# Score matmuls of a decode-attention kernel: 24 written-out matmuls a half against two register-addressed loops

## The chip, the cores and the metric

The kernel runs on one core of a Trainium2 chip. The metric is device time in microseconds (us) from the first to the last instruction of the program on that core; three timed runs of the kernel before gave 1981.87, 1982.41 and 1983.38 us. The engines that matter here are TensorE (PE in the profile; PEld is its weight loads), VectorE (DVE), ScalarE (ACT) and SyncE (SP), which issues nearly all the transfers. Each engine has its own instruction stream, and the streams meet only through semaphores.

## The reference: four layers of one-token attention

One token of width 640 goes through four attention layers, A, B, A, B, each with a residual. A layer normalises the token, projects it to 32 query heads of 192, scores each query against 8192 cached keys, takes a softmax, sums the cached values with these weights, and projects back to 640. All inputs are bf16.

```python
def _B_ref(x, k_cache, v_cache, wq, wo):
    q = (x @ wq).reshape(B, Sq, H, Dh).transpose(0, 2, 1, 3)
    scores = einsum("bhqd,bhkd->bhqk", q, k_cache) * (Dh ** -0.5)
    p = softmax(scores, axis=-1)
    o = einsum("bhqk,bhkd->bhqd", p, v_cache)
    return o.transpose(0, 2, 1, 3).reshape(B, Sq, H * Dh) @ wo

x = x + _A_ref(layernorm(x), ...)
x = x + _B_ref(layernorm(x), ...)
x = x + _A_ref(layernorm(x), ...)
x = x + _B_ref(layernorm(x), ...)
```

The A and the B caches are each 32 heads x 8192 rows x 192 numbers for keys and the same for values. All of it is read once per layer, apart from a few tensors kept on the core, so the kernel moves about 849 MB.

## The kernel before

**Tiling.** Heads are taken two at a time: 16 pairs a layer, 64 in all. A pair's keys are one 128-partition tile of 128 rows x 192 numbers per partition (64 partitions for each head), and so are its values. Each is split in two halves, u = 0 and u = 1, of 3.1 MB. Halves live in a pool of eight slots on the core. A planner in Python lists all transfers in order (`plan`), picks the slots that come free earliest, and makes each transfer wait on SP's queue for the last reader of its slot. Most keys and values come as one transfer of 6.3 MB into two neighbouring slots.

**The work of a pair**, in the order of the list `steps`:

- `products(p, u)` for both halves. VectorE multiplies the key half in place by the query, in four quarters of 48 of the 192 columns (line 599, "pool <- pool, q_sb"). TensorE then sums the products over the 192 columns, eight columns at a time: 24 matmuls against an identity matrix, each 128 x 512, added up in the PSUM bank S0 or S1. The first is an ordinary `matmul` (line 612), which also loads the identity as weights; the other 23 go through the helper `matmul_held` (line 58), which keeps the weights that are loaded. The first six wait for quarter 0 (`PE.wait(chunks[0])`), the next six for quarter 1, and so on. The last one signals a semaphore, which frees the slot of the key half and releases the reduction.
- `softmax(p)`. VectorE reduces the eight columns left in S0 and S1 (line 621), takes the maximum (lines 623 and 630, with a small TensorE matmul at line 626 between them), and ScalarE takes the exponentials (line 636).
- `values(p)`. TensorE multiplies the weights by the value tile, 48 matmuls with 16 weight columns each, in four column groups (lines 678 and 58), into the accumulator O.
- `gather(p)`. VectorE adds up eight slices of O (lines 696 and 697), TensorE folds the partitions (line 710), and ScalarE writes the pair's output row (line 721).

**Order.** The streams are written out by hand, and each engine does its part strictly in that order. On VectorE the next pair's products come after this pair's `gather`, which waits for this pair's `values`, which waits for this pair's score matmuls. On TensorE the score matmuls of u = 1 come after those of u = 0. So a pair is one chain through VectorE, TensorE, VectorE, ScalarE, TensorE and VectorE, and pairs do not overlap except in their transfers. Every five pairs, output weights `wo` are applied (line 538), and between layers the query weights `wq` are.

**The queue object.** `Queue.op` adds an instruction to an engine's stream, with its waits ahead of it; with `signal=False` no semaphore is signalled. `emit` plays the list to the engine.

Of the kernel before, what the change touches and what calls it, by code (L numbers as in the profile page):

```python
# [55 lines left out]
def matmul_held(t, out, lhsT, rhs, start, stop, size=128, column=0):  # L56

    return t.add_instruction(mybir.InstMatmult(  # L58
        name=t.bass.get_next_instruction_name(), engine=mybir.EngineType.PE,
        ins=[t.lower_ap(rhs), t.lower_ap(lhsT, for_matmul_weights=True)], outs=[t.lower_ap(out)],  # L60
        start_tensor_calc=start, stop_tensor_calc=stop, tile_size=(128, size), tile_position=(0, column), ldweights=False))
# [7 lines left out]
def build(nc, A_x, A_k, A_v, A_wq, A_wo, B_x, B_k, B_v, B_wq, B_wo, out):  # L69
    _, H, SK, DH = A_k.shape  # L70
# [8 lines left out]
    QD = DH // 4  # L79
    R = 512 // JU  # L80
# [17 lines left out]
    with ExitStack() as ctx:  # L98
        def sb(name, shape, dt):
            return ctx.enter_context(nc.sbuf_tensor(name, shape, dt))  # L100
# [4 lines left out]
        def sem(name):  # L105
            return ctx.enter_context(nc.semaphore(name))

        ident = sb("ident", [P, P], BF16)
# [51 lines left out]
        Su = [(use["S0"],), (use["S1"],)]  # L160
# [6 lines left out]
        PE = Queue(sem("pPE"))  # L167
# [7 lines left out]
        e = PO.op(lambda g: g.memset(ident[:], 0.0))  # L175
# [6 lines left out]
        e = PO.op(lambda g: g.memset(mask, 0.0))  # L182
        for t in range(G):
            e = PO.op(lambda g, t=t: g.affine_select(
                out=mask, in_=mask, compare_op=ALU.not_equal, fill=1.0,
                base=-32 * t, pattern=[[-1, 2], [-2, VK]], channel_multiplier=1), e)
# [13 lines left out]
        def first_load(kind, l, p):  # L200

            n = (kind, pair(l, p))
            if l >= 2 and n in KEPT[l - 2]:
                return (l - 2, ORDER[l - 2]["pairs"].index(n[1]))
            return (l, p)

        def stays(kind, l, p):
            return l < 2 and (kind, pair(l, p)) in KEPT[l]
# [17 lines left out]
        for l in range(NL):  # L226
# [8 lines left out]
            for p in range(NPAIR):  # L235
# [17 lines left out]
                if p < NPAIR - 2:  # L253
# [8 lines left out]
                    if p + 1 in (PAIRS_W, 2 * PAIRS_W):  # L262
                        b = (p + 1) // PAIRS_W - 1
# [132 lines left out]
        def need(n):  # L396

            while n not in landed:
                m = plan[issued[0]]
                issued[0] += 1  # L400
                landed[m] = transfer(m)
            return landed[n]
# [45 lines left out]
        def layer(l, ev_z, ev_true):  # L448
# [7 lines left out]
            if l == 2:  # L456
                busy(2)
            e = DV.op(lambda v: v.scalar_tensor_tensor(out=nv[:], in0=mv[:, 0:1], scalar=mv[:, 0:1], in1=mv[:, 1:2],
                                                       op0=ALU.mult, op1=ALU.subtract))
            e = DV.op(lambda v: v.tensor_scalar(vs[:], nv[:], -float(DH), float(DH) * EPS, ALU.mult, ALU.add), e, last["rs"])  # L460
# [6 lines left out]
            if l < 2:  # L467
                e = need(("wq", l, 0))
# [4 lines left out]
            else:  # L473
                e = ev_first[l - 2]
                q_first = wq0[l - 2]
            PE.wait(e)
            for c in range(DC):
                for h in range(2):
                    e = PE.op(lambda t, c=c, h=h: t.matmul(
                        QM[64 * h:64 * h + 64, 0:DH], lhsT=xb[:, c:c + 1].broadcast_to([P, 64]),  # L480
                        rhs=q_first[:, c, h * DH:(h + 1) * DH], start=(c == 0), stop=(c == DC - 1)),
                        signal=(c == DC - 1 and h == 1), bank=QMu)
# [106 lines left out]
            def products(p, u):  # L589
                nk = ("k",) + first_load("k", l, p) + (u,)  # L590
                nt = ("t", l, p, u) if stays("k", l, p) else nk
                kin = slot[place[nk]].rearrange("p (j d) -> p j d", d=DH)
                k3 = slot[place[nt]].rearrange("p (j d) -> p j d", d=DH)
                qi = (l * NPAIR + p) % 2
                DV.wait(need(nk), need(nt), ev_q[p])
                chunks = []
                for c in range(4):
                    d0 = c * QD
                    e = DV.op(lambda v, d0=d0: v.tensor_tensor(  # L599
                        k3[:, :, d0:d0 + QD], kin[:, :, d0:d0 + QD],  # L600
                        q_sb[qi][:, d0:d0 + QD].unsqueeze(1).broadcast_to([P, JU, QD]), ALU.mult))
                    chunks.append(e)
                last["q"][qi] = chunks[-1]
                S = SP_[u]
                PE.wait(last["S"][u], ev_const)
                for c in range(4):
                    PE.wait(chunks[c])
                    for r in range(QD // R):
                        d0 = c * QD + r * R
                        fin = c == 3 and r == QD // R - 1  # L610
                        e = PE.op(lambda t, d0=d0, fin=fin: (
                            t.matmul(S[:, :], lhsT=ident[:], rhs=k3[:, :, d0:d0 + R], start=True, stop=fin) if d0 == 0 else  # L612
                            matmul_held(t, S[:, :], ident[:], k3[:, :, d0:d0 + R], False, fin)), signal=fin, bank=Su[u])
                freed[nt] = ev_S[p, u] = e

            def softmax(p):
# [109 lines left out]
            for n in [n for n in steps if n[1] == l]:  # L726
                if n[0] == "m":
                    products(*n[2:])
                elif n[0] == "s":
                    softmax(n[2])  # L730
# [36 lines left out]
            if l + 1 == NL:  # L767
                a = slot[place[("wo", 3, 2)]][0:33, 0:HD]
                return a, AC.op(lambda c: c.activation(a, YR, ACT.Copy), ev_y, last["oT"], bank=YBu)
            ev_z = DV.op(lambda v: v.tensor_tensor(z[:], xc[:], YB[:, 0:DC], ALU.add), ev_y, ev_xc, bank=YBu)  # L770
            e = DV.op(lambda v: v.tensor_tensor(x_true[:], x_true[:], YB[:, 0:DC], ALU.add), ev_y, ev_true, bank=YBu)
# [5 lines left out]
        e = SP.op(lambda s: s.dma_start(out[0, 0].rearrange("(h n) -> h n", h=2), ev_z[0:33:32, :]), ev_true, sem=semOUT, inc=16)  # L777
# [54 lines left out]
```

## Time and profile before

| What | Value |
|---|---|
| median of three timed runs | 1982.41 us |
| profiled execution, its span | 1982.1 us |
| DMA queue q1, share of 16 DMA engines over the span | 99.6 % |
| HBM read, mean rate | 848.36 MB, 428 GB/s |
| VectorE busy | 1201.2 us (61 %) |
| TensorE matmul busy | 1288.6 us (65 %) |
| ScalarE busy | 139.9 us (7 %) |
| products on VectorE, line 599 | 512 of 1753 ns, 861.1 us |
| score matmuls, lines 612 and 58 | 3072, 851.3 us busy |

The busy shares are averages, and a matmul's end is modelled, so that 65 % for TensorE is not a measure of how near it is to its limit. The waits between engines, and the times at which one pair's instructions follow another's, say more. In the profile's lists, an arrow "<-" in a group's name stands between what is written and what is read; after a wait it stands ahead of what ended it. An engine with a q after its name is that engine's sequencer, the part that reads instructions and handles moves, branches and semaphores itself.

### The profile page before, as it was taken

What the parts mean: (1) busy time and instruction counts of PE and PEld (TensorE: products, weight loads), DVE (VectorE), ACT (ScalarE), POOL (GpSimd) and SP (SyncE); (2) the same over time, 40 slices, a digit from 0 to 9 for tenths busy, and PEclk for the clock granted to TensorE, in tenths of its full rate; (3) what the DMA queues carried; (4) which work ended last, traced back from release to release, by engine and by line L of the source; (5) the groups of instructions that cost most, each with busy time, mean ns of one, the idle gap of its engine ahead of it and who ended that gap; (6) DMA issues with size and microseconds to landing.
All of it is one profiled execution on the core that took longest, in us unless ns stands there. A gap on an engine that the chain in (4) does not pass through costs nothing.

```text
span 1982.1 us, 13748 instructions
## 1 busy us (share of the span) xinstructions
PE 1288.6 (65%) x8248; PEld 146.4 (7%) x3160; DVE 1201.2 (61%) x1376; ACT 139.9 (7%) x462; POOL 4.5 (0%) x23
## 2 busy tenths in 40 slices
PE   3567476666466666666785676675776766657658
PEld 0001001000100100100020010010001001000001
DVE  3566467467166657556745565665764775665656
ACT  0000000000000000000010000000000100000000
POOL 0000000000000000000000000000000000000000
PEclk9787776778677777777887877878787888777779
DMA  9999999999999999999999999999999999999998
GB/s 414 438 431 430 431 436 432 430 430 429 435 432 433 434 430 432 429 435 433 426 407 426 425 426 426 432 430 431 434 429 427 435 431 433 433 432 431 433 433 367
DMA packets 26930, 849.25 MB, mean 428 GB/s; under 512 B 3058, under 2 KB 3188, under 8 KB 3828
## 3 DMA queue, kind: packets, MB, share of 16 engines
q1 hardware_dynamic: 26724, 848.38, 99.6%
q8 instruction: 45, 0.74, 0.2%
q14 instruction: 17, 0.14, 0.0%
q10 hardware_dynamic: 144, 0.00, 0.0%
HBM read 848.36 MB, written 0.00 MB: 428 GB/s over the span
## 4 chain that ended last, share of the span: by engine, by line
DMA 67%; DVE 17%; PE 15%; ACT 1%; issue 0%; SPq 0%
DMA pool<-in_B_k_cache_dram 27%; DMA pool<-in_A_v_cache_dram 20%; DVE pool L599 15%; DMA pool<-in_A_k_cache_dram 14%; PE S L58 6%; DMA pool<-in_B_v_cache_dram 6%; PE OY L58 5%; PE OY L678 3%; DVE acc L697 1%; ACT p_sb L636 1%; DVE s_sb L621 1%; PE S L612 0%; DVE m_bf L623 0%; PE OY L538 0%; PE QM L626 0%
## 5 line engine op out<-in xcount | busy, mean ns | idle before, releaser
L599 DVE TENSOR_TENSOR pool<-pool,q_sb 128x3072 bf16<-128x3072 bf16 x512 | 861.1, 1753 | 229.5 <-DMA pool<-in_B_k_cache_dram 133.5
L58 PE MATMUL S<-pool,ident 128*128 128x512 bf16 x2944 | 789.5, 425 | 19.5 <-DVE pool L599 17.6
L710 PE MATMUL TB<-acc,small 128*1 128x192 f32 x240 | 82.7, 495 | 212.0 <-DVE acc L697 212.0
L58 PE MATMUL OY<-pool,p_sb 128*16 128x512 bf16 x1920 | 202.7, 498 | 0.0
L696 DVE TENSOR_SCALAR acc<-OY,small 128x192 f32<-128x192 f32 x64 | 26.7, 418 | 287.5 <-PE OY L58 256.3
L678 PE MATMUL OY<-pool,p_sb 128*16 128x512 bf16 (+1 forms) x1216 | 148.2, 495 | 69.5 <-DMA pool<-in_A_v_cache_dram 63.5
L612 PE MATMUL S<-pool,ident 128*128 128x512 bf16 x128 | 61.8, 483 | 201.3 <-DVE pool L599 201.2
L697 DVE SCALAR_TENSOR_TENSOR acc<-OY,small,acc 128x192 f32<-128x192 f32 x424 | 177.1, 418 | 14.9
L621 DVE TENSOR_REDUCE s_sb<-S 128x64 f32<-128x512 f32 x128 | 88.0, 688 | 69.7 <-PE S L58 69.7
L527 ACT ACTIVATE q_sb<-QM 128x192 bf16<-128x192 f32 x60 | 19.9, 331 | 944.0 <-PE QM L521 944.0
L721 ACT ACTIVATE rows<-TB,small 1x192 bf16<-1x192 f32 x120 | 43.2, 406 | 596.3 <-PE TB L710 596.3
L692 DVE RECIPROCAL small<-TB 1x2 f32<-1x2 f32 x64 | 11.2, 175 | 94.5 <-PE TB L651 75.3
L636 ACT ACTIVATE p_sb<-s_sb,small 64x128 bf16<-64x128 f32 x128 | 55.7, 435 | 161.2 <-DVE small L630 160.4
L612 PEld LDWEIGHTS S<-pool,ident 128*128 128x128 bf16 x128 | 12.9, 101 | 676.2 <-DVE pool L599 604.4
L651 PE MATMUL TB<-small,ones 128*1 128x2 f32 x120 | 11.4, 165 | 74.1 <-ACT p_sb L636 74.1
L678 PEld LDWEIGHTS OY<-pool,p_sb 128*16 128x16 bf16 (+1 forms) x1216 | 39.8, 107 | 217.3 <-issue 138.8
L626 PE MATMUL QM<-ident,m_bf 128*64 128x64 bf16 x128 | 14.0, 216 | 54.4 <-DVE m_bf L623 53.9
L710 PEld LDWEIGHTS TB<-acc,small 128*1 128x1 f32 x240 | 19.8, 101 | 310.8 <-DVE acc L697 284.0
L630 DVE TENSOR_REDUCE small<-QM 128x1 f32<-128x64 f32 x64 | 14.4, 225 | 35.2 <-PE QM L626 35.2
L521 PEld LDWEIGHTS QM<-rows,one_b 1*64 1x64 bf16 x120 | 6.2, 100 | 347.0 <-issue 341.1
L538 PE MATMUL OY<-oT,pool 128*128 128x1 bf16 x675 | 28.6, 178 | 1.9 <-ACT oT L584 1.9
L538 PEld LDWEIGHTS OY<-oT,pool 128*128 128x128 bf16 x675 | 27.8, 131 | 3.8 <-ACT oT L584 2.5
(74 smaller groups left out, 215.2 us busy)
## 6 DMA issues: line engine op xcount, KB each, us to landing
pool<-in_B_k_cache_dram SPq DMA_DIRECT2D x28, 6144.0 KB, 37.9
pool<-in_B_v_cache_dram SPq DMA_DIRECT2D x28, 6144.0 KB, 33.5
pool<-in_A_v_cache_dram SPq DMA_DIRECT2D x27, 6144.0 KB, 27.5
pool<-in_A_k_cache_dram SPq DMA_DIRECT2D x34, 3072.0 KB, 20.5
pool<-in_A_k_cache_dram SPq DMA_DIRECT2D x14, 6144.0 KB, 36.4
pool<-in_A_v_cache_dram SPq DMA_DIRECT2D x10, 3072.0 KB, 14.7
pool<-in_B_k_cache_dram SPq DMA_DIRECT2D x8, 3072.0 KB, 22.5
pool<-in_A_wo_dram SPq DMA_DIRECT2D x6, 2400.0 KB, 21.9
```

The lines of the kernel that those rows point to most:

```text
L58: return t.add_instruction(mybir.InstMatmult(name=t.bass.get_next_instruction_name(), engine=mybir.EngineType.PE, ins=[t.lower_ap(rhs), t. ...
L527: lambda a: a.activation(q_sb[i][:], QM[:, 0:DH], ACT.Copy), e, last["q"][i], bank=QMu)
L538: e = PE.op(lambda t, i=i, c=c, f=y_first[0], fin=n[0] == "wol" and i == k - 1: t.matmul(YB[:, c:c + 1], lhsT=t3[:, i, c:D:DC], rhs=o[:, i ...
L599: e = DV.op(lambda v, d0=d0: v.tensor_tensor(k3[:, :, d0:d0 + QD], kin[:, :, d0:d0 + QD], q_sb[qi][:, d0:d0 + QD].unsqueeze(1).broadcast_t ...
L612: t.matmul(S[:, :], lhsT=ident[:], rhs=k3[:, :, d0:d0 + R], start=True, stop=fin) if d0 == 0 else
L621: lambda v, u=u: v.tensor_reduce(s[:, u * JU:(u + 1) * JU], SP_[u][:].rearrange("p (j r) -> p j r", r=R), AX.X, ALU.add), ev_S[p, u], last ...
L636: ev_p[p] = AC.op(lambda a, h=h, r=r: a.activation(p_sb[par][r, :, h], s[r, :], ACT.Exp, bias=negm[par][r, 0:1], accum_out=l_col[par][r, h ...
L678: t.matmul(o, lhsT=x, rhs=y, start=f, stop=fin) if c == 0 else
L696: v.tensor_scalar(acc[:], O[:, 0:DH], pick[:, 0:1], None, ALU.mult) if i == 0 else
L697: v.scalar_tensor_tensor(out=acc[:], in0=O[:, i * DH:(i + 1) * DH], scalar=pick[:, i:i + 1], in1=acc[:], op0=ALU.mult, op1=ALU.add)), e if ...
L710: e = PE.op(lambda t, h=h: t.matmul(TB[96:97, C_O + h * DH:C_O + (h + 1) * DH], lhsT=half[:, h:h + 1], rhs=acc[:], start=True, stop=True), ...
L721: last["TO"] = last["row_written"] = AC.op(lambda a, h=h: a.activation(orow[:, o0 + h * DH:o0 + (h + 1) * DH], TB[96:97, C_O + h * DH:C_O ...
```

## The change

In `products`, the 24 score matmuls of a half are written as two loops that run on TensorE's own sequencer. The first part does the ordinary first matmul (columns 0 to 7) and then a loop of 11 turns, for columns 8 to 95; the second part is a loop of 11 turns for columns 96 to 183 and one last matmul that ends the accumulation and signals. One turn holds one `matmul_held` whose moving operand is addressed by a register. There are two waits instead of four: the first part waits for quarter 1 (`chunks[1]`), the second for quarter 3 (`chunks[3]`). The number of matmuls, their operands and their order stay the same.

```diff
                 PE.wait(last["S"][u], ev_const)
-                for c in range(4):
-                    PE.wait(chunks[c])
-                    for r in range(QD // R):
-                        d0 = c * QD + r * R
-                        fin = c == 3 and r == QD // R - 1
-                        e = PE.op(lambda t, d0=d0, fin=fin: (
-                            t.matmul(S[:, :], lhsT=ident[:], rhs=k3[:, :, d0:d0 + R], start=True, stop=fin) if d0 == 0 else
-                            matmul_held(t, S[:, :], ident[:], k3[:, :, d0:d0 + R], False, fin)), signal=fin, bank=Su[u])
+                def scores(t, a, b):
+
+                    def one(d, start, stop):
+                        x = k3[:, :, bass.ds(d, R)]
+                        if start:
+                            return t.matmul(S[:, :], lhsT=ident[:], rhs=x, start=True, stop=stop)
+                        return matmul_held(t, S[:, :], ident[:], x, False, stop)
+
+                    if a == 0:
+                        one(0, True, False)
+                        a = R
+                    end = b - R if b == DH else b
+                    with t.Fori(a, end, R) as d:
+                        one(d, False, False)
+                    return one(end, False, True) if b == DH else None
+
+                PE.wait(chunks[1])
+                PE.op(lambda t: scores(t, 0, DH // 2), signal=False, bank=Su[u])
+                PE.wait(chunks[3])
+                e = PE.op(lambda t: scores(t, DH // 2, DH), bank=Su[u])
                 freed[nt] = ev_S[p, u] = e
```

Built into instructions, a turn of the loop is four on TensorE's stream: one that does four register operations at once (it works out the operand's address), the matmul, a register addition (the loop's counter), and a compare-and-branch. Ahead of each loop stand a register move, which sets the counter, and a branch. In the second part the wait for quarter 3 sits on that register move. The written-out form has a plain matmul for each of them and nothing else. The program has 256 such loops: two for each of 128 halves. The streams of the other engines are the same as before.

## The prediction

> **What bounds the kernel now.** I read the page first, then the waits, then the timeline of one pair, then the rows of the sequencers. The page's top, slices and queues:
>
> ```profile
> span 1982.1 us, 13748 instructions
> ...
> DMA  9999999999999999999999999999999999999998
> ...
> q1 hardware_dynamic: 26724, 848.38, 99.6%
> q8 instruction: 45, 0.74, 0.2%
> ```
>
> The transfers are the bound: their engines are busy in every fortieth of the span, 99.6% overall. Nothing in the change moves fewer bytes of data, so the kernel can only stay or lose. What it can absorb is read from the view of waits, in the rows where compute waits for a transfer (total us, times, longest):
>
> ```profile
> DVE pool L599 <- DMA pool<-in_B_k_cache_dram: 133.5, 30, 13.4
> DVE pool L599 <- DMA pool<-in_A_k_cache_dram: 94.6, 27, 9.8
> ...
> PE OY L678 <- DMA pool<-in_A_v_cache_dram: 63.5, 21, 10.9
> ...
> PE QM L479 <- DMA pool<-in_B_wq_dram: 12.8, 1, 12.8
> ...
> PE OY L678 <- DMA pool<-in_B_v_cache_dram: 6.0, 4, 3.5
> ```
>
> That is 310 us of slack, about 4.8 us for each of 64 pairs. The timeline shows how one pair looks where no transfer is waited for (start us, us):
>
> ```profile
> 1572.85 13.43 DVE L599 TENSOR_TENSOR pool<-pool,q_sb 128x3072 bf16<-128x3072 bf16 x8
> ...
> 1575.06 6.94 PE L58 MATMUL S<-pool,ident 128*128 128x512 bf16 x23
> ...
> 1586.34 1.46 PE L58 MATMUL S<-pool,ident 128*128 128x512 bf16 x6 [0.21 <-DVE pool L599]
> ...
> 1587.83 0.69 DVE L621 TENSOR_REDUCE s_sb<-S 128x64 f32<-128x512 f32 x1 [0.94 <-PE S L58]
> ...
> 1592.63 0.63 PE L58 MATMUL OY<-pool,p_sb 128*16 128x512 bf16 x8
> ...
> 1593.76 3.13 DVE L697 SCALAR_TENSOR_TENSOR acc<-OY,small,acc 128x192 f32<-128x192 f32 x7
> 1596.81 1.75 DVE L599 TENSOR_TENSOR pool<-pool,q_sb 128x3072 bf16<-128x3072 bf16 x1
> ```
>
> From products to next products it takes 23.96 us, all one chain. In the steady stretch where transfers set the pace, successive pairs start at 721.80 and 750.85 us, 29.05 apart: 5.1 us of slack, which agrees with the sum above. The last six score matmuls end 1.52 us after the products (1587.80 against 1586.28). TensorE now keeps up with VectorE: 6 matmuls take under the 1.68 us of a quarter. The spacing of those six is (1.46 - 0.39) / 5 = 0.21 us, 0.39 being the length of one.
>
> **The change, part by part.**
>
> *Matmuls.* The same 24 a half; their time on the array, 0.21 us each at full clock, does not change.
>
> *Fewer waits.* The first part begins after quarter 1 (3.36 us into the products) instead of quarter 0 (1.68). For the first half of a pair this costs nothing: until then the sequencer can have queued the turns behind the waiting first matmul, and 12 matmuls of 0.21 us fit before quarter 3 is done at 6.72 us. The second part's wait is on a register move, which the sequencer does itself. So nothing behind it is queued until then: not the turns, not the second half's loops, not the query spread or the maximum. VectorE's reductions and, through softmax, values and gather, the next pair's products wait behind that. From 6.72 us on, 33 turns have to be issued one after the other (11 of half 0, 22 of half 1). If a turn takes more than 0.28 us, the data of half 1 (13.44 us) are always there first, and the turn alone sets the end.
>
> *The turn.* The trace of before has no such loop, so its price is bounded from rows of sequencer work elsewhere (median ns in the middle; the engine's name has a q):
>
> ```profile
> L184 POOLq MOVE  x4: 29/29/29, 1.7 to 2.7; - x4
> ```
> ```profile
> L98 SPq COMPARE_BRANCH  x1: 33/33/33, 1981.8 to 1981.8; - x1
> ```
> ```profile
> L49 PEldq EVENT_SEMAPHORE  x81: 51/51/51, 3.7 to 1978.9; - x81
> L49 ACTq EVENT_SEMAPHORE  x71: 17/17/17487, 26.2 to 1971.2; - x71
> ```
>
> Low end: durations alone. Move 0.029 twice (for the fused register operations and for the addition), branch 0.033, and a matmul 0.02 (75 pairs of weight load and matmul of line 538 take 3.08 us, so 0.041 a pair): 0.11 us. That hides behind the array's 0.21. Middle: from one start to the next. The unrounded starts put 0.111 us from a move to the instruction behind it and 0.165 from the compare-and-branch to the drain behind it: 0.111 + 0.02 + 0.111 + 0.165 = 0.407 us. High: TensorE's sequencer takes 51 ns for a semaphore event where ScalarE's takes 17; 0.034 more on three instructions gives 0.509. The farthest is all four at the branch's 0.165, as a matmul with a register address is no plain one: 0.66. I take 0.407, as it counts what a sequencer needs until its next instruction, and keep 0.21 and 0.66.
>
> *The sum.* From quarter 3 on: 33 turns x 0.407 = 13.43; three loop entries' branches and two more moves, 3 x 0.165 + 2 x 0.111 = 0.72; three plain matmuls' issue and the last one's run, 0.06 + 0.39 = 0.45. Together 14.60 us; 6.72 + 14.60 = 21.32 us after the pair's start, 7.88 after the products (13.44). Before it was 1.52, so 6.36 us more a pair, 407 us for 64. Of the 310 us of slack some stays: the 9.8 of the first keys, which wait for the start, and an estimated half of the 10.9 and 12.8 at layer ends, where transfers are ordered late. That leaves about 289. New time: 1982.1 + 407 - 289 = 2100 us. The profiled execution's 1982.1 stands 0.3 under the median of 1982.41, so nothing is added. In general 0.01 us of turn is 33 x 64 x 0.01 = 21 us, and the slack is used up at 289 / 64 = 4.5 us more a pair, a turn of 0.35 us.
>
> *What goes.* 768 waits become 512, and 1280 TensorE instructions fewer are stored. Instruction fetches are 0.74 MB of 849, so the gain is under 0.09%, 1.7 us, and I cost it at nothing.
>
> *Two rules weighed.* The trace's only compare-and-branch took 33 ns, and 165 until the next instruction. The Trainium skill, "Advanced Engine Details and Errata", section Control Flow Timing, gives about 108 ns for it. By that the turn is an estimated 0.35 us and the sum 1982 to 1985 us; no run so far shows which is right.
> The profile has 45 instruction packets in all. The Trainium skill, "Runtime: NRT & Kernel Launch", section Instruction fetch mechanics, speaks against the change: a taken branch out of the fetched window has to wait for a fetch. A loop of four instructions should lie inside it; no row shows a taken branch.
>
> **The rivals.**
>
> *Not slower.* The sequencer issues a turn in 0.35 us or less, so the slack covers it. For it speak the durations (0.11 us by the low end) and that TensorE takes plain instructions at 0.02 us; against it the gaps behind moves and branches. Time: 1982 us, the transfers' own. It decides at 0.35 us a turn. That the loops do nothing new, because the queue always runs ahead, is the same case: the register move's wait speaks against it.
>
> *A much dearer turn.* A turn of 0.57 us or more: TensorE's sequencer is slow throughout, as its semaphore event hints, or a taken branch refills. At 0.66: 0.253 x 33 = 8.35 us more a pair, 2100 + 534 = 2634 us. A fetch at each loop entry would be a kin: 0.2% of 16 engines' 1982 us over 45 packets is about 1.4 us, times 3 entries times 64 = 270 us, so 2370.
>
> *The clock falls.* With a matmul each 0.41 us the array is 52% busy instead of 76% (1.28 of 1.68). The clock halves after idle stretches now (0.74 granted in the pair from 721.80, 0.86 in the one above without waits). At half clock a matmul takes 0.43 us, which sets the turn, and the value rounds take 1.28 us instead of 0.85 (both are seen before): 33 x 0.02 + 4 x 0.43 = 2.4 us a pair, 2100 + 152 = 2252 us. Against it: at full clock 52% may well be enough.
>
> **How the numbers follow.** Dearer turn than 0.35 but under 0.57 us, with or without the clock: 0.60, likeliest 2100 us, its own range 1990 to 2450 (0.01 us is 21 us: 0.57 gives 2442). Not slower: 0.20. Much dearer: 0.18. Faster by some side effect of a shorter program: 0.02. What a measurement of this kernel can tell from no change is about 0.2%, 4 us. The range takes in the not-slower case and ends where the much dearer one begins: 1978 to 2450, with some 0.82 in it. Slower is 0.60 + 0.18, and the "same" 0.20 is the rival's.
>
> **What would show it.** Right: TensorE's stream has score matmuls a constant 0.4 us apart from 6.7 us after a pair's start on; the second S reduction starts some 8 us after the products end instead of 1.55; VectorE's wait for "PE S" grows from 69.7 us to some 470; its waits for keys shrink to a few; the DMA share falls to some 94%, with gaps in the slices. Wrong: turns at 0.21 to 0.35 us and DMA still at 99%; turns over 0.57; gaps at each loop's first turn rather than between turns (fetches); granted clock near 0.5 through the scores. The size hangs on one number that the trace doesn't show, the turn.

## The result and the profile after

The changed kernel takes 2401.79 us (median of five runs, 2393.18 to 2409.89) against 1982.08 for the kernel before: 1.212 times as long, 95 % interval 1.209 to 1.214. The direction was forecast and the time lies inside the forecast range, but the likeliest value, 2100 us, was 118 us over the kernel before, and the change cost 420.

The profiled execution of the changed kernel has a span of 2390.7 us. The page's top, the slices and the queue, to be held against the same lines of before:

```profile
span 2390.7 us, 22452 instructions
...
DMA  9987987987888888888689989889879978888982
...
q1 hardware_dynamic: 26724, 848.38, 84.6%
```

The transfers moved as many bytes but were no longer busy throughout; they now wait longer for slots (SyncE's largest wait for the score sums grew from 726.6 to 909.8 us). The chain of waits says who sets the pace instead (shares of the span by engine, before and after):

```profile
DMA 67%; DVE 17%; PE 15%; ACT 1%; issue 0%; SPq 0%
```
```profile
PE 64%; DVE 19%; issue 10%; DMA 4%; ACT 3%; SPq 0%
```

Transfers made up 67 % of that chain before and make up 4 % now. In the view of waits (total us, times, longest us) one row took the place of the others; it stands first as it was before, then with the rows of after:

```profile
DVE s_sb L621 <- PE S L58: 69.7, 64, 3.6
```
```profile
DVE s_sb L633 <- PE S L58: 714.3, 127, 12.8
...
DVE pool L599 <- DMA pool<-in_B_k_cache_dram: 21.4, 3, 13.4
...
DVE pool L599 <- DMA pool<-in_A_k_cache_dram: 15.9, 6, 9.8
...
PE QM L479 <- DMA pool<-in_B_wq_dram: 9.5, 1, 9.5
...
PE OY L690 <- DMA pool<-in_A_v_cache_dram: 7.2, 2, 5.5
```

VectorE's wait for the score sums grew from 69.7 to 714.3 us; the first half's sums now make it wait too (127 times instead of 64). What compute waits for transfers shrank from 310 to 54 us (21.4 + 15.9 + 9.5 + 7.2). The timeline of one pair (start us, us), to be read against the pair of before that starts at 1572.85 us:

```profile
1293.86 13.43 DVE L599 TENSOR_TENSOR pool<-pool,q_sb 128x3072 bf16<-128x3072 bf16 x8
...
1297.33 0.61 PE L611 MATMUL S<-pool,ident 128*128 128x512 bf16 x1 [2.52 <-DVE pool L599]
1297.73 10.47 PE L58 MATMUL S<-pool,ident 128*128 x23
...
1308.04 0.38 PE L611 MATMUL S<-pool,ident 128*128 128x512 bf16 x1
...
1308.26 10.51 PE L58 MATMUL S<-pool,ident 128*128 x23
...
1318.80 0.69 DVE L633 TENSOR_REDUCE s_sb<-S 128x64 f32<-128x512 f32 x1 [9.87 <-PE S L58]
...
1324.73 3.14 DVE L709 SCALAR_TENSOR_TENSOR acc<-OY,small,acc 128x192 f32<-128x192 f32 x7
1327.79 1.75 DVE L599 TENSOR_TENSOR pool<-pool,q_sb 128x3072 bf16<-128x3072 bf16 x1
```

The products still take 13.43 us. The 23 matmuls of a half take 10.5 us instead of 6.9 in half 0 and 5.7 in half 1. Half 1 comes after half 0 as before, and so starts 14.2 us into the pair instead of 9.0: the second reduction starts 11.5 us after the products (1318.80 against 1307.29) instead of 1.55. From products to next products it is 33.93 us instead of 23.96. The 9.97 us between them are the growth of that delay; softmax, values and gather are as before. Neither pair waits for a transfer: what was 5.1 us shorter than the transfers' 29.05 us a pair is now 4.9 us longer.

The source view of the loop's line shows what TensorE's sequencer does (ns: shortest, median, longest):

```profile
L618 PEldq FUSED_REGOPS  x2816: 44/53/58, 39.8 to 2368.4; - x188
L618 PEldq ALU_OP  x2816: 36/36/42, 40.0 to 2368.5; - x188
L618 PEldq COMPARE_BRANCH  x2816: 76/208/341, 40.1 to 2368.6; - x188
L618 PEldq MOVE  x256: 29/29/29, 39.7 to 2363.5; - x128
```

Durations alone sum to 0.30 us a turn. From start to start, by the unrounded starts in the trace (medians), it is more: 0.112 us from the register operations to the addition (the matmul's issue lies between), 0.097 from the addition to the branch, 0.266 from the branch back to the register operations. The median turn takes 0.474 us; a fifth of them take over 0.5, and the mean is 0.486. At full clock a matmul takes 0.215 us on the array, so TensorE is then idle for over half of each turn.

### The profile page after: what moved, and what is told of

It reads as the page before. It is cut to its first block, busy times and chain, and to the rows that moved or that the text cites. A ratio compares the mean times of both kernels' runs of the same rounds, so it can differ in the third digit from the quotient of the medians.

```text
span 2390.7 us, 22452 instructions
## 1 busy us (share of the span) xinstructions
PE 1638.6 (69%) x8248; PEld 147.5 (6%) x3160; DVE 1202.4 (50%) x1376; ACT 140.3 (6%) x462; POOL 4.5 (0%) x23
## 3 DMA queue, kind: packets, MB, share of 16 engines
q1 hardware_dynamic: 26724, 848.38, 84.6%
## 4 chain that ended last, share of the span: by engine, by line
PE 64%; DVE 19%; issue 10%; DMA 4%; ACT 3%; SPq 0%
PE S L58 46%; DVE pool L599 8%; DVE acc L709 7%; PE OY L58 7%; PE OY L690 4%; ACT p_sb L648 2%; PE S L611 2%; DMA pool<-in_B_k_cache_dram 2%; DVE s_sb L633 2%; DMA pool<-in_A_k_cache_dram 1%; PE OY L538 1%; DVE acc L708 1%; DVE m_bf L635 1%; PE TB L722 1%; PE QM L638 1%
## 5 line engine op out<-in xcount | busy, mean ns | idle before, releaser
L58 PE MATMUL S<-pool,ident 128*128 (+1 forms) x2944 | 1129.8, 423 | 209.5 <-issue 8.5
L599 DVE TENSOR_TENSOR pool<-pool,q_sb 128x3072 bf16<-128x3072 bf16 x512 | 860.0, 1753 | 38.7 <-DMA pool<-in_B_k_cache_dram 21.4
L633 DVE TENSOR_REDUCE s_sb<-S 128x64 f32<-128x512 f32 x128 | 88.6, 692 | 714.3 <-PE S L58 714.3
L58 PE MATMUL OY<-pool,p_sb 128*16 128x512 bf16 x1920 | 216.1, 527 | 0.0
L690 PE MATMUL OY<-pool,p_sb 128*16 128x512 bf16 (+1 forms) x1216 | 154.3, 511 | 7.2 <-DMA pool<-in_A_v_cache_dram 7.2
L611 PE MATMUL S<-pool,ident 128*128 128x512 bf16 x128 | 62.3, 486 | 136.0 <-DVE pool L599 136.0
```

The source lines that it names most:

```text
L58: return t.add_instruction(mybir.InstMatmult(name=t.bass.get_next_instruction_name(), engine=mybir.EngineType.PE, ins=[t.lower_ap(rhs), t. ...
L599: e = DV.op(lambda v, d0=d0: v.tensor_tensor(k3[:, :, d0:d0 + QD], kin[:, :, d0:d0 + QD], q_sb[qi][:, d0:d0 + QD].unsqueeze(1).broadcast_t ...
L611: return t.matmul(S[:, :], lhsT=ident[:], rhs=x, start=True, stop=stop)
L633: lambda v, u=u: v.tensor_reduce(s[:, u * JU:(u + 1) * JU], SP_[u][:].rearrange("p (j r) -> p j r", r=R), AX.X, ALU.add), ev_S[p, u], last ...
L690: t.matmul(o, lhsT=x, rhs=y, start=f, stop=fin) if c == 0 else
```

## The experiments

In all of them theory A is that the loops' issue on TensorE's sequencer is the cost, and that it counts only as far as it delays the second reduction beyond what the transfers' slack absorbs. "Lateness" below is how much later that reduction starts after the products than in the kernel before, as a mean over the 64 pairs, from the starts in the trace (1.69 us before, 11.85 after: lateness 10.16). Edits are shortened, and shown against the changed kernel. The first four runs shared a chip and 15 runs of the kernel before (1982.2 us), the last two another and seven runs (1982.34 us).

**The two waits without the loops.**

```diff
+for c in (1, 3):
+    PE.wait(chunks[c])
+    for d0 in range((c - 1) * QD, (c + 1) * QD, R):
+        ... the plain matmul at d0, as before
-PE.wait(chunks[1]); PE.op(lambda t: scores(t, 0, DH // 2), ...)
-PE.wait(chunks[3]); e = PE.op(lambda t: scores(t, DH // 2, DH), ...)
```

> The two coarser waits alone: 24 written-out matmuls a half, the first 12 behind quarter 1, the last 12 behind quarter 3, no loop. Theory A (the loops' issue on TensorE's sequencer is the cost): after the products 12 matmuls of 0.21 us remain instead of 6, so the second S reduction starts about 2.8 us after the products instead of 1.55; 1.3 us a pair lie inside the slack of some 4 us a pair, and the time stays at 1982 us within 4. Theory B (the late start is a good part of the cost): the time rises by 50 us or more, up to 64 x 1.3 = 83 us, 2065.

Measured: 1986.97 us, 1.0022 times before (1.0013 to 1.0031). The reduction starts 2.84 us after the products in the median pair, as expected. The time is 4.8 us more, just over the 4 allowed for: a tenth of what theory B needs at least. So the waits by themselves, without loops, are about 1 % of the 420 us.

**The loops without the two waits.**

```diff
+for c in range(4):
+    PE.wait(chunks[c])
+    e = PE.op(lambda t, c=c: scores(t, c * QD, (c + 1) * QD), signal=c == 3, bank=Su[u])
-PE.wait(chunks[1]); PE.op(lambda t: scores(t, 0, DH // 2), ...)
-PE.wait(chunks[3]); e = PE.op(lambda t: scores(t, DH // 2, DH), ...)
```

> The loops alone, with the four waits of before: one loop a quarter (5, 6, 6 and 5 turns), 44 turns a pair as in the changed kernel, but 8 loop entries instead of 4. If the sequencer does not go past a matmul that waits (so the loops start when the first wait ends), the first loop starts 1.8 us into the products instead of 3.47 and the chain ends about 1.65 us earlier, less some 0.2 us for each of four more entries: 0.8 us a pair, 50 us, about 2350. If it runs ahead and only the last waits count, nothing is gained and the entries cost 64 x 0.8 = 50: about 2450.

Measured: 2293.83 us, 1.157 times (1.155 to 1.159), 108 us below the changed kernel. The timeline of one pair:

```profile
172.16 13.43 DVE L599 TENSOR_TENSOR pool<-pool,q_sb 128x3072 bf16<-128x3072 bf16 x8
...
173.96 0.61 PE L611 MATMUL S<-pool,ident 128*128 128x512 bf16 x1 [0.23 <-DVE pool L599]
174.36 10.39 PE L58 MATMUL S<-pool,ident 128*128 x23
...
184.59 0.38 PE L611 MATMUL S<-pool,ident 128*128 128x512 bf16 x1
184.80 10.40 PE L58 MATMUL S<-pool,ident 128*128 x23
...
195.24 0.69 DVE L632 TENSOR_REDUCE s_sb<-S 128x64 f32<-128x512 f32 x1 [9.05 <-PE S L58]
```

The first matmul starts 1.80 us into the products instead of 3.47, and the whole row of turns moves with it, to the end. So the start of the first loop counts, which it could not if its turns had been queued ahead. With the loops in place the two coarser waits thus cost 108 us, though without loops they cost 5: here they come on top of a delay that has used the slack up. The gain was twice the forecast one, as an entry costs nothing extra here: leaving a loop and entering the next takes 0.134 + 0.088 us, less than a taken branch's 0.266.

**Two matmuls a turn.**

```diff
-    with t.Fori(a, end, R) as d:
-        one(d, False, False)
+    with t.Fori(a, end, 2 * R) as d:
+        one(d, False, False)
+        one(d + R, False, False)
```

Two plain matmuls stand before the first loop and two after the second, instead of one.

> Two matmuls a turn, two waits as in the changed kernel: 20 turns a pair instead of 44, 8 plain matmuls instead of 4. Theory A: a turn grows by one set of register operations with its matmul, 0.474 + 0.11 = 0.585 us; 3.47 + 20 x 0.585 + 4 x 0.22 + 8 x 0.21 = 17.7 us to the last matmul's start, 4.6 us after the products to the reduction; 3.1 us more a pair than before lie inside the slack, so 1982 to 2000 us. Theory D (the register-addressed matmul is what is slow, not the branch): 40 of 44 such matmuls are still there and the time stays above 2300 us.

Measured: 1990.99 us, 1.0046 times (1.0031 to 1.0062), where theory A put it. A turn takes 0.117 + 0.104 (an address for each matmul) + 0.097 + 0.266 = 0.584 us, and the reduction starts 3.67 us after the products in the median pair. That is 0.9 us earlier than worked out. The sum had charged the entries and the plain matmuls too much: the earlier loops are through before the last one's data are there (its register move runs at 13.48 us, just after the products' end), so only that loop lies behind the products. Its queue row:

```profile
q1 hardware_dynamic: 26724, 848.38, 99.4%
```

Forty register-addressed matmuls a pair are left, and the transfers are the bound again: fewer than half as many turns, with as many fewer additions and branches, gave back 411 of the 420 us.

**A fixed address in the loop.**

```diff
     with t.Fori(a, end, R) as d:
-        one(d, False, False)
+        one(a, False, False)
```

> The same loops, but the matmul in a loop has a fixed address (it sums one eight-column block over and over, so ten of eleven blocks of each loop are left out of the scores); the fused register operations go, the counter and the branch stay. Theory A: the branch (0.27 us from its start to the next turn) and the counter (0.10) remain, a turn of 0.38 to 0.42 us; 44 turns give 2.4 to 4.1 us a pair less, 2140 to 2250 us. Theory D (the register address is the cost): turns at the array's 0.21 us and about 1985 us.

Measured: 2076.92 us, 1.047 times (1.046 to 1.049). The turn is 0.097 + 0.266 = 0.363 us: the addition and the branch cost as much as in the changed kernel, and the matmul fits beside them. I had expected 0.38 to 0.42 and so 2140 us at best. The source view of the loop's line in this kernel lists no register operations:

```profile
L618 PEldq ALU_OP  x2816: 36/36/42, 40.1 to 2054.5; - x188
L618 PEldq COMPARE_BRANCH  x2816: 76/208/343, 40.2 to 2054.6; - x188
L618 PEldq MOVE  x256: 29/29/33, 40.0 to 2050.8; - x128
```

So of 0.474 us a turn, 0.112 belong to the register address together with the matmul's issue, and the other 0.36 to counting and branching. These, with the two coarser waits still there, keep the kernel 95 us slower.

**Loops in one half only.** The same number of turns, at two places.

```diff
+if u == 1:      # the other run: u == 0
+    ... 24 plain matmuls behind four waits, as before
+else:
     PE.wait(chunks[1])
     PE.op(lambda t: scores(t, 0, DH // 2), signal=False, bank=Su[u])
     PE.wait(chunks[3])
     e = PE.op(lambda t: scores(t, DH // 2, DH), bank=Su[u])
```

> Loops in half 0 of every pair, half 1 written out with its four waits as before. Theory A (22 turns of 0.474 us from 3.47 us on, then half 1's 24 matmuls behind them at 0.215 us): half 0 ends 14.0 us into the pair, half 1 at 19.6, so the second S reduction starts 6.2 us after the products, 4.65 more than before. With the law read from the runs so far (time = 1982 + 64 x (lateness - 3.72) us): 1982 + 60 = 2041 us. If instead the loops' cost were per loop turn alone wherever it lies (half of the changed kernel's 419 us): 2190 us.

> Loops in half 1 of every pair, half 0 written out. As many turns as with loops in half 0. Theory A: the first loop begins at quarter 1 of half 1, 10.2 us into the pair, 22 turns and two loop entries end at 21.1, the reduction starts 8.1 us after the products, 6.5 more than before, and the time is 1982 + 64 x 2.8 = 2162 us, some 120 us over the kernel with loops in half 0 though the turns are as many. If the cost were per turn wherever it lies: the same as with loops in half 0.

Measured: 2055.43 us with loops in half 0 (1.037 times, 1.035 to 1.039) and 2144.11 us in half 1 (1.080 times, 1.079 to 1.082). Equal turns, 89 us apart. In the median pair half 0's loops run from 3.5 to 14.0 us and start 21 of their 22 turns before the products end at 13.4; half 1's run from 10.1 to 20.6 us and start only 7 before that. VectorE's waits for the sums differ by about as much (94 us), first with loops in half 0, then in half 1:

```profile
DVE s_sb L643 <- PE S L58: 364.7, 127, 7.1
```
```profile
DVE s_sb L643 <- PE S L58: 458.2, 67, 9.7
```

The forecast 2041 and 2162 us were 14 too low and 18 too high.

**All runs on one line.** For each profiled execution, how far its span is over the 1982.1 us of before, per pair, and what the slack absorbed:

| Kernel | lateness, us | span over before, us | the same / 64 | absorbed, us a pair |
|---|---|---|---|---|
| two waits, written out | 1.47 | 3.9 | 0.06 | 1.41 |
| two a turn | 2.13 | 4.7 | 0.07 | 2.06 |
| loops in half 0 | 4.70 | 71.4 | 1.12 | 3.58 |
| fixed address | 5.20 | 94.6 | 1.48 | 3.72 |
| loops in half 1 | 6.08 | 166.2 | 2.60 | 3.48 |
| four loops | 8.59 | 304.7 | 4.76 | 3.83 |
| the changed kernel | 10.16 | 408.6 | 6.38 | 3.78 |

The last five absorb 3.5 to 3.8 us a pair; every microsecond beyond that costs about 64. (Runs of one kernel lie up to 17 us apart, 0.26 us a pair, so differences between these five mean little.) Below it almost nothing is paid, but not quite nothing: 3.9 us at a lateness of 1.47. Where those few come from was not tested.

## Why the prediction was right and wrong

Right: the bound before, the way the cost arises (issue on the sequencer, then VectorE late, then transfers waiting for slots) and the kind of its signs, the wait for "PE S" above all. Their sizes were too small: that wait is 714 us, not some 470, and the DMA share 84.6%, not some 94. The score loops' regular spacing is there, and there are no gaps at loop entries that would speak of fetches. The program needs fewer fetches (38 packets on the main fetch queue instead of 45, and 17 on a second one in both) and gains nothing visible from it. The size was wrong, and the steps that failed are three terms of the sum; the second was also wrong in its mechanism:

- **The turn** was put at 0.407 us and is 0.474. The address work with the matmul's issue was 0.131 and is 0.112, the addition 0.111 and is 0.097; the compare-and-branch was 0.165 and is 0.266. The row that it came from was a branch of another engine at the program's end, with no sign of whether it was taken. On TensorE a branch that falls through lasts 0.076 us and needs 0.134 until the next instruction, a taken one 0.208 and 0.266. 33 turns x 0.067 x 64 = 141 us.
- **"The sequencer can have queued the turns behind the waiting first matmul"** was wrong, and with it the start at 6.72 us with 33 turns. The register move ahead of the first loop carries no wait of its own, yet in none of the 64 pairs did it run before quarter 1 was done; in 55 it ran 0.05 us after. In the other nine the quarter had long been done and the array was still at earlier matmuls; there the move ran 0.66 to 2.6 us before the first score matmul started. So the sequencer went on past a matmul that only waited for the array, and not past one that waited for its semaphore. 44 turns in a row begin at 3.47 us, and the run with four loops, which begins them at 1.80, is faster by as much. Eleven more turns, begun 3.25 us earlier, are 11 x 0.474 - 3.25 = 1.96 us a pair, 126 us. Smaller items take back 24: the branch charged at each loop entry has no record in the trace (the first register operations start 0.088 us after the move), while some turns and pairs are longer. That makes up the rest of the lateness: 10.16 - 6.36 = 3.80 us a pair, 243 us in all, so 102 beside the turn's 141.
- **The slack** was put at 289 us. The waits for transfers shrank by 256, and the net absorption is 64 x 10.16 - 408.6 = 242 us, 14 less. Some 8 of these are value sums that grew: in the 56 pairs away from the layer ends they take 4.53 us instead of 4.38, at a granted clock of 0.66 instead of 0.72. What the others are was not found. The forecast was 47 us too high.

Together 118 + 141 + 102 + 47 = 408 us, the 408.6 between the profiled spans. That the time still fell inside the range was luck: the sum with the true turn gives 2241 us, and the two other terms, for which the range had no room of their own, add the rest.

Of the rivals, "not slower" needed a turn of 0.35 us; even without a register address it is 0.363. "Much dearer" needed 0.57. "The clock falls" is refuted by the stage's own clock (stretch, its length, busy us of PE, PEld, DVE, ACT and POOL with counts, granted clock, DMA share, GB/s):

```profile
1300.00:1318.40 18.40, 15.26 (x43) 0.10 (x1) 7.97 (x6) 0.00 (x0) 0.00 (x0) 0.93 1.00 431
1318.40:1335.00 16.60, 8.77 (x69) 1.15 (x27) 11.85 (x17) 2.04 (x7) 0.00 (x0) 0.74 1.00 416
```

It is 0.93 through this stretch of turns (0.88 from the first score matmul at 1297.33 us on), and 0.82 over the whole span against 0.78 before. Where the clock is halved, at the start of that pair, score matmuls lie 0.427 us apart, which still fits into a turn of 0.474. The rival's price was also misread: at full clock a value round takes 0.65 us (starts at 1591.12 and 1591.77 in the pair before the change), not 0.85, so it would have been some 50 us dearer.

The branch was the disputed rule. The taken branch took 0.208 us here, about twice the 108 ns that the Trainium skill, "Advanced Engine Details and Errata", section Control Flow Timing, gives for a compare-and-branch; the untaken one, 0.076, is below it. The measurement decides: for a loop the taken one counts, with 0.266 us to the next instruction.

The same page, section Sequencer Loop, says that an engine instruction is pushed into a queue and that it waits for semaphore readiness. Read alone, this suggests that the sequencer goes on past it, as I had assumed; the register moves here show that a register instruction behind a waiting matmul does not run until the wait ends.

## What to carry to other kernels

A loop on an engine's sequencer costs its turn, here 0.474 us of which 0.36 are counting and branching, against 0.215 us for the matmul inside it: put enough work into a turn that the engine is the slower of the two, or at least that the turns fit into the slack, as two matmuls a turn did (0.43 us of work in 0.584). Where transfers are the bound, read how far the compute chain of one tile is from the transfers' time for a tile, and expect an extra delay to be free up to somewhat less than that (here 5.1 us by that reading, 3.5 to 3.8 in the runs), and to cost its full length times the number of tiles beyond it. Do not count on register work being done ahead of a wait: look at which instruction waits, and start the loop's clock there.

## What was unexpected of the hardware

- A register move without a wait of its own, behind a matmul that waits for a semaphore, ran only after that wait in all 64 pairs, 0.05 us after it in 55 of them. In the other nine the matmul waited only for the array, and the move ran 0.66 us or more ahead of it.
- A taken compare-and-branch on TensorE needed 0.266 us until the next instruction; leaving one loop and entering the next needed 0.134 + 0.088 = 0.222, less than staying in.
- With a matmul of 0.215 us in every 0.474 us, TensorE kept its full clock nearly throughout: between the products' end and the second reduction the granted clock was 0.99 on average.
